# Linear attention and channel mix on one core: pairs of batches against single batches with quarter-tile projections

## Chip, cores, metric

One core of one Trainium2 chip. The time is device microseconds of one execution, as a median of several; the profile is one execution of the same program, and "span" is its length without the fixed cost around it (about 2 us less than the time: 107.7 against 109.86). "Slow" is here a run over 1.5% above the fastest of the same kernel.

## The reference, cut to what matters

```python
# B=4, H=4, S=1088, D=32, r=8; d_model=128, d_ff=1024
def phi(x):                                   # sketch features, 64 per token and head
    a = einsum('rd,bhsd->bhsr', S1, x)
    b = einsum('rd,bhsd->bhsr', S2, x)
    return einsum('bhsi,bhsj->bhsij', a, b).reshape(..., r * r)
q_p, k_p = phi(q), phi(k)
kv, z = einsum('bhsf,bhsd->bhfd', k_p, v), k_p.sum(axis=2)
x = (q_p @ kv) / (q_p @ z + 1e-6)             # heads side by side: (B, S, 128)
xk = mu_k * x + (1 - mu_k) * x_prev           # x_prev: the token before
xr = mu_r * x + (1 - mu_r) * x_prev
out = sigmoid(xr @ w_r) * (relu(xk @ w_k) ** 2 @ w_v)
```

Nothing of q can be finished for a batch before all of its k and v have been summed. So there is an opening (k projection, k features, accumulation of kv and z, q projection, q features, numerators) before the first matmul of the channel mix ("the MLP").

## The kernel before: the parts that matter

The four batches are worked in two halves of two. A tile is 128 rows: two batches by 64 tokens. The k projection is one 128 x 128 by 64-column fp32 matmul per tile, the q projection two half-array ones. The accumulation of kv uses quarters of the array (64 x 64).

```python
def k_proj(half, gi):
    ...
    for t in range(t1 - t0):
        nc.tensor.matmul(p[:, t * 64:t * 64 + 64], kT[half][:, t0 + t, :], SW[:, 0, :, :2, :], ...)

def q_proj(g):
    ...
    for t in range(qn[g]):
        for b2 in range(2):
            nc.tensor.matmul(p[64 * b2:64 * b2 + 64, t * 96:t * 96 + 96], qT[half][:, T, 64 * b2:64 * b2 + 64],
                             SW[:, 2 * half + b2]..., tile_position=(0, 64 * b2))
```

k of the first half and q of the second are transposed on VectorE, the other two on TensorE, after a regrouping on ScalarE. PSUM is four rings of two. A list scheduler in the program orders all pieces; it is told when each load arrives. "Spins" are matmuls of zeros, put there in the hope that they keep the TensorE clock from being lowered.

```python
arrive = {"S": 4.6, "k00": 5.5, "k01": 5.5, "v0": 8.5, "k1": 11.5, "q0": 14.5, "v1": 17.5, "q10": 20.0, "q11": 22.0, "w": 27.0}
...
def spin(count):
    for _ in range(count):
        nc.tensor.matmul(zps[:, 0, :], zero[:, :P], zero[:], skip_group_check=True)
spin(7)   # ... and spin(12) after the small matmuls that prepare the sketch weights
```

## Time and profile before

| | before |
|---|---|
| time, median of the rounds beside the changed kernel | 108.06 us (later rounds: 106.8 to 107.2) |
| span of the profiled run | 107.7 us |
| first MLP matmul starts at (timeline) | 52.1 us |
| from there to the end | 55.6 us |

The profiled run before took 109.86 us and is slow.

TensorE has one hole, and the clock falls twice, near 20 and near 30 to 36 us. The hole, in the timeline of the kernel before (start, length, engine, line, operation, count, and the idle time before it with what ended it): ScalarE waits for a load, TensorE for ScalarE.

```profile
15.24 1.16 PE L227 MATMUL kv<-tok_v_66,kp 64*64 64x64 f32 x64
19.32 1.14 ACT L182 COPY tall<-tok_k_68 128x512 f32<-128x512 f32 x2 [5.05 <-DMA tok_k_68<-in_k_dram]
19.99 1.11 PE L187 MATMUL tp<-ident,tall 128*128 128x128 f32 x4 [3.59 <-ACT tall L182]
```

The table by windows of the kernel before, cut where the first MLP matmul starts. Columns: window, length, busy us of PE, PEld, DVE, ACT and POOL, each with its records, then granted clock, DMA share, GB/s.

```profile
0.00:30.00 30.00, 23.75 (x368) 17.22 (x368) 13.78 (x35) 7.45 (x17) 8.30 (x21) 0.94 0.89 236
30.00:52.10 22.10, 20.39 (x411) 17.53 (x413) 17.31 (x37) 12.47 (x31) 2.31 (x13) 0.85 0.12 13
52.10:107.70 55.60, 50.82 (x586) 36.83 (x594) 46.73 (x90) 50.37 (x78) 0.00 (x0) 1.00 0.12 42
```

Before the MLP, VectorE and ScalarE are idle half of the time; after it PE and ACT are full. This is the room that the change goes after.

### The profile page before, as it was taken

To read this page: it belongs to the slowest core of one execution; us is meant where nothing else is said; L and a number is where in the kernel's file an instruction comes from. 1 tells how busy PE (TensorE), PEld (TensorE's weight loads), DVE (VectorE), ACT (ScalarE), POOL (GpSimd) and SP (SyncE) were. 2 spreads that over 40 slices of the span, in tenths; PEclk is the share of its full clock that TensorE was granted. 3 is DMA by queue.
4 is the path that set the end of the run, shared out by engine and by line. 5 is a ranking of instruction groups with operands and counts; after the bars stand their busy time and mean duration, and the time that the engine had idled before them with its cause. 6 is when DMAs were issued, how large, how long until landed. Compare 5 with 4: busy or idle time off the path is not lost.

```text
span 107.7 us, 3217 instructions
## 1 busy us (share of the span) xinstructions
PE 95.0 (88%) x1365; PEld 71.6 (66%) x1375; DVE 77.8 (72%) x160; ACT 70.3 (65%) x124; POOL 10.6 (10%) x33
## 2 busy tenths in 40 slices
PE   5999990598789999976999999999999999999850
PEld 2445990487679889754667687776866776677720
DVE  3275690123549796949999998599997997878770
ACT  0500410830293533767699999989999998999940
POOL 7050000007790000000000000000000000000000
PEclk9999999679955699999999999999999999999999
DMA  0999999994990000000000000200202002122221
GB/s 10 343 293 366 279 280 287 209 272 159 127 98 0 0 6 6 3 6 0 3 0 6 0 0 0 97 6 0 97 6 97 0 8 90 30 73 97 97 100 53
DMA packets 6157, 9.70 MB, mean 90 GB/s; under 512 B 1520, under 2 KB 2416, under 8 KB 6144
## 3 DMA queue, kind: packets, MB, share of 16 engines
q1 hardware_dynamic: 3360, 6.13, 18.9%
q0 software_dynamic: 1952, 1.71, 8.7%
q10 hardware_dynamic: 832, 1.67, 4.9%
q8 instruction: 11, 0.18, 0.7%
q14 instruction: 2, 0.02, 0.1%
HBM read 7.80 MB, written 2.23 MB: 93 GB/s over the span
## 4 chain that ended last, share of the span: by engine, by line
PE 50%; DMA 19%; ACT 13%; issue 5%; POOL 4%; DVE 3%; SPq 3%; ACTq 0%; POOLq 0%
DMA tok_v_67<-in_v_dram 19%; PE o L419 10%; PE h L398 8%; PE xps L361 8%; PE qtp L323 7%; PE abwp L294 7%; PE tp L187 3%; PE kv L227 3%; PE abp L198 2%; SPq L71 2%; ACT r L435 1%; ACT PP_179 L379 1%; DVE osb L440 1%; ACT k_1507 L404 1%; PE rps L427 1%
## 5 line engine op out<-in xcount | busy, mean ns | idle before, releaser
L398 PE MATMUL h<-XK,wk 128*128 128x512 bf16 (+1 forms) x62 | 17.6, 366 | 0.2
L206 DVE TENSOR_TENSOR kp<-ab 128x1024 f32<-128x1024 f32 (+1 forms) x10 | 10.4, 1060 | 6.5 <-ACT ab L168 6.5
L187 PE MATMUL tp<-ident,tall 128*128 128x128 f32 x34 | 6.9, 340 | 4.1 <-ACT tall L182 4.1
L323 PE MATMUL qtp<-ident,qp 128*128 128x128 f32 x68 | 9.4, 275 | 1.1 <-ACT abw L168 1.0
L206 DVE TENSOR_TENSOR qp<-abw,an 128x1024 f32<-128x1024 f32 (+1 forms) x9 | 10.3, 1154 | 0.0
L168 ACT COPY qpT<-qtp 128x512 f32<-128x512 f32 x15 | 8.3, 601 | 2.4 <-PE qtp L323 2.3
L361 PE MATMUL xps<-qpT,kvbd 128*64 128x256 f32 (+3 forms) x80 | 9.3, 358 | 0.5 <-ACT qpT L168 0.5
L84 PE MATMUL zps<-zero 128*128 128x512 bf16 x19 | 7.6, 578 | 1.3 <-POOL zero L79 1.3
L323 PEld LDWEIGHTS qtp<-ident,qp 128*128 128x128 f32 x68 | 7.4, 142 | 1.6 <-ACT abw L168 1.2
L168 ACT COPY ab<-abp 128x256 f32<-128x256 f32 (+1 forms) x8 | 2.8, 352 | 8.8 <-PE abp L198 8.7
L187 PEld LDWEIGHTS tp<-ident,tall 128*128 128x128 f32 x34 | 4.7, 172 | 4.9 <-ACT tall L182 4.3
L398 PEld LDWEIGHTS <-wk 128*128 128x128 bf16 x72 | 5.8, 98 | 2.5 <-issue 1.0
L361 PEld LDWEIGHTS xps<-qpT,kvbd 128*64 128x64 f32 x80 | 4.5, 136 | 3.2 <-ACT qpT L168 0.7
L198 PE MATMUL abp<-SW,kT_160 128*128 128x64 f32 x34 | 5.5, 304 | 1.0 <-issue 1.0
L440 DVE TENSOR_TENSOR osb<-o,r 128x512 f32<-128x512 f32 (+1 forms) x9 | 5.9, 655 | 0.5 <-PE o L419 0.5
L198 PEld LDWEIGHTS abp<-SW,kT_160 128*128 128x128 f32 x34 | 5.1, 225 | 1.6 <-issue 1.6
L182 ACT COPY tall<-tok_k_68 128x512 f32<-128x512 f32 (+1 forms) x5 | 2.7, 556 | 5.1 <-DMA tok_k_68<-in_k_dram 5.1
L227 PE MATMUL kv<-tok_v_66,kp 64*64 64x64 f32 x272 | 5.9, 244 | 0.0
L84 PEld LDWEIGHTS <-zero 128*128 128x128 bf16 x19 | 2.4, 135 | 5.3 <-issue 3.6
L227 PEld LDWEIGHTS kv<-tok_v_66,kp 64*64 64x64 f32 x272 | 5.2, 155 | 0.8 <-DVE kp L206 0.3
L435 ACT ACTIVATE r<-rps 128x512 f32<-128x512 f32 (+1 forms) x9 | 5.5, 610 | 0.0
L168 ACT COPY abw<-abwp 128x384 f32<-128x384 f32 x6 | 2.9, 482 | 3.4 <-PE abwp L294 3.4
(246 smaller groups left out, 220.2 us busy)
## 6 DMA issues: line engine op xcount, KB each, us to landing
out_dram<-osb SPq DMA_DIRECT2D x7, 256.0 KB, 2.0
hd_k_70<-in_k_dram SPq DMA_DIRECT2D x1, 544.0 KB, 4.0
hd_k_71<-in_k_dram ACTq DMA_DIRECT2D x1, 544.0 KB, 6.0
tok_v_66<-in_v_dram SPq DMA_DIRECT2D x1, 544.0 KB, 8.6
tok_v_66<-in_v_dram ACTq DMA_DIRECT2D x1, 544.0 KB, 9.3
tok_k_68<-in_k_dram SPq DMA_DIRECT2D x1, 544.0 KB, 14.5
tok_k_68<-in_k_dram ACTq DMA_DIRECT2D x1, 544.0 KB, 16.5
tok_q_69<-in_q_dram SPq DMA_DIRECT2D x1, 544.0 KB
```

The lines of the kernel that those rows point to most:

```text
L84: nc.tensor.matmul(zps[:, 0, :], zero[:, :P], zero[:], skip_group_check=True)
L168: nc.scalar.copy(o, i)
L187: nc.tensor.transpose(tp[:, t * P:t * P + P], tall[x, t0][:, t].rearrange("p h d -> p (h d)"), ident[:])
L198: nc.tensor.matmul(p[:, t * 64:t * 64 + 64], kT[half][:, t0 + t, :], SW[:, 0, :, :2, :], skip_group_check=True)
L206: nc.vector.tensor_mul(o, _ap(a_, list(a_.ap[1:]) + [[0, R]]), _ap(b_, list(b_.ap[1:3]) + [[0, R]] + [b_.ap[3]]))
L227: nc.tensor.matmul(kv[hp:hp + 64, b2, (h // 2) * 64:(h // 2) * 64 + 64], f[rows, t - t0, h].rearrange("p i j -> p (i j)"), _ap(rhs, [[(H - ...
L294: nc.tensor.matmul(p[64 * b2:64 * b2 + 64, t * 96:t * 96 + 96], qT[half][:, T, 64 * b2:64 * b2 + 64], SW[:, 2 * half + b2].rearrange("p h ...
L323: nc.tensor.transpose(p[:, t * P:t * P + P], qp[g][:, t, 2 * pair:2 * pair + 2].rearrange("p h i j -> p (h i j)"), ident[:])
L361: nc.tensor.matmul(o[64 * pair:64 * pair + 64], kvbd[:, 2 * half + b2, pair, :], qpT[g, pair][:].rearrange("p t (b s) -> p t b s", b=2)[:, ...
L398: nc.tensor.matmul(h[:, c, :n * P], wk[:, cp, c * P:c * P + P], XK[:, 4 * g:4 * g + n, :].rearrange("p t s -> p (t s)"))
L419: nc.tensor.matmul(bank["o", g][:, t * P:t * P + P], k2[:, c, t * P:t * P + P], wv[:, 2 * cp + c, :], start=(cp == 0 and c == 0 and t == 0 ...
L440: nc.vector.tensor_mul(o[:, :n].rearrange("p t f -> p (t f)"), bank.pop(("o", g))[:, :n * P], rs[g][:, :n * P])
```

## The change

Its intent: work batch by batch, so that the first MLP matmul needs the three loads of one batch and not those of both halves; no TensorE transposes of inputs; a q or k projection cut into quarter-array matmuls, meant to run side by side; PSUM as eight single banks, each piece placed by hand; and 18 spins in places where TensorE was expected to wait. The order of all pieces is a fixed list.

```diff
-    zps = psum.tile([P, 2, 512], F32, name="zps", tag="h")
-    def spin(count):
+    banks = [psum.tile([P, 512], F32, name=f"bank{i}", tag=f"bank{i}") for i in range(8)]
+    def spin(i, count):
...
+    load_v(0)
+    load_kq("q", 0)
+    for b in range(1, B):
+        load_kq("k", b)
+        load_v(b)
+        load_kq("q", b)
...
-    spin(12)
+    spin(0, 5)
...
-        for t in range(t1 - t0):
-            nc.tensor.matmul(p[:, t * 64:t * 64 + 64], kT[half][:, t0 + t, :], SW[:, 0, :, :2, :], skip_group_check=True)
+    def k_proj(b, t0, t1):
+        for t in range(t0, t1):
+            for y in range(2):
+                rows = slice(64 * y, 64 * y + 64)
+                for x in range(2):
+                    nc.tensor.matmul(bank("ab", b, t0, y)[64 * x:64 * x + 64, (t - t0) * 16:(t - t0) * 16 + 16],
+                                     kqT["k", b][rows, t, :], SW[rows, 0, x, :2, :],
+                                     skip_group_check=True, tile_position=(64 * y, 64 * x))
...   (q_proj likewise, 24 columns)
+    ORDER = """
+        tk.0.0.0 tk.0.1.0 kpj.0.0@01 tk.0.0.9 tk.0.1.9 kpj.0.9@23 kab.0.0.0:DVE kab.0.9.1:ACT kab.0.0.1:DVE
+        kab.0.9.0:ACT kp.0.0 spin.6@4 kacc.0.0@45 kp.0.9 kacc.0.9 tk.1.0.0 tk.1.1.0 kpj.1.0@67 tq.0.0.A tq.0.1.A
+        tq.0.1.B kz.0 tq.0.0.B kab.1.0.0:ACT kab.1.0.1:ACT kkv.0 kw.0@0 ksw.0 spin.2@1 q1.0.8@13 q1.0.0@26 qab.0.0.0:ACT
...   (some 40 lines more)
```

In fp32 each of these matmuls is four records on TensorE (two weight loads, two matmuls).

## The prediction

> **What bounds it now.** Engine sums of the page: PE 95.0 us busy, DVE 77.8, ACT 70.3 of a 107.7 us span. Three stages (table by windows, timeline):
> - 0 to 30 us, opening. First K-projection at 10.0 us; PE has nothing from 16.4 to 20.0 us (ACT waits 5.1 us for the second k load), DVE is busy 13.8 of 30 us. Loads cover pairs of batches; the last holds the weights back (POOL waits 17.2 us, issues them at 25 to 28 us). The chain of waits gives that load 19%.
> - 30 to 52 us: both attention halves stand before the MLP. Granted clock 0.84, then 0.67 (20 to 40 us): 64 accumulation records take 1.9 us cold, 1.09 warm. First MLP matmul at 52.1 us.
> - 52 to 104.5 us, steady: PE 50.9 and ACT 50.4 of 52.5 us, DVE 46.4; PE and ACT limit it together, PSUM in rings of two. PE durations overlap, so its 97% is not peak.
>
> **Removed.** 34 PE transposes of k1/q0 (warm 110 ns each by spacing, 3.7 us), ten ACT regroupings (about 4.5 us), ten evacuations (2.5 us ACT, 2.8 DVE). Denominators go from 9 to 5 calls (DVE -2.8). Four squares leave DVE (-2.5) for ACT (+3.7).
>
> **Added.** DVE transposes for the other four batch tensors: +3.3 us. More q evacuations on DVE: +4.5. ACT: 72 half-size relus instead of 36, but back-to-back copies start 0.48 us apart at 512 columns and relus 0.91 at 1024, so only +1.6; more edge pieces, +2.5. Projections: 272 quarter-tile matmuls, two records each, for k and for q. [...] Quarter tiles overlap: the accumulation runs 17 ns a record. At 17 each projection set costs 9.2 us[...]. Spins: 19 become 30; the 18 late ones stand before known waits and keep the clock.
>
> Sums afterwards: ACT about 65, DVE 78, useful PE 80 to 86 us warm. No engine loses much work; the gain is overlap.
>
> **Critical path.** Batch 0 needs three loads (about 1.7 us each at the 290 to 340 GB/s of the DMA row). Walking the order with trace durations (estimate): k projection at 8 us, accumulation done 14, q projection 16.5 to 19, first features 22.5, first numerator 25, x_mix 30, first MLP matmul at 31 to 33 us instead of 52. Then remain PE 55 to 60, DVE 55, ACT 54 us. They balance; with 90 to 95% kept they end near 93 to 95, plus the last MLP chain and store: span 96.
>
> **Prediction: 97.5 us, 8 in 10 within 92 to 103.** Faster by over 2%: 0.93; within 2%: 0.05; slower: 0.02.
>
> **What will show it.** First relu near 32 us; weights issued by about 15 us; granted clock near 1.0 from 12 to 40 us; projection sets of 136 records in 2.3 to 3.7 us; DVE busiest or level with PE, above 85% from 15 us on; ACT no longer saturated.
>
> **What would make it wrong.** Quarter-tile projections whose neighbours share array rows (the accumulation alternates rows) not overlapping:[...] time 105 or above. A fixed order whose guesses are off[...]. DVE transposes of 544 columns costing more than the 0.5 us I extrapolate. The other way: a steady stage without ring waits could run at 97% and give 92.

In the trace of the kernel before, warm, the k projections of all four batches are 68 matmul records 101 to 110 ns apart, 6.9 to 7.5 us, and the q projections 136 records 42.3 ns apart, 5.8 us. The forecast of time is no sum of these terms: the walk to a first MLP matmul at 31 to 33 us, then 55 to 60 us of the busiest engine at 90 to 95%, then the last chain and store, came to a span of 96 us and a time of 97.5. The 80 to 86 us of useful PE contain the projections. The 0.5 us for a transpose of 544 columns is an estimate from the kernel before (0.38 us at 256 columns, 0.40 at 288); the changed kernel took 0.68 us.

## More of the kernel before

The page of the kernel before: busy sums, TensorE's busy tenths in 40 slices of 2.7 us, the granted clock in tenths, and two of the DMA queues (packets, MB, share of 16 engines).

```profile
PE 95.0 (88%) x1365; PEld 71.6 (66%) x1375; DVE 77.8 (72%) x160; ACT 70.3 (65%) x124; POOL 10.6 (10%) x33
...
PE   5999990598789999976999999999999999999850
...
PEclk9999999679955699999999999999999999999999
...
q1 hardware_dynamic: 3360, 6.13, 18.9%
...
q8 instruction: 11, 0.18, 0.7%
```

## The result

| | before | after |
|---|---|---|
| time, median (range) | 108.06 us (107.15 to 110.02) | 120.3 us (119.71 to 121.44) |
| ratio of fast runs | | 1.1177, interval 1.1025 to 1.1328 |
| span of the profile | 107.7 us | 118.5 us |
| first MLP matmul | 52.1 us (a slow run; 48.6 in the fast run of before_kv) | 50.2 us (predicted 31 to 33) |
| from there to the end | 55.6 us | 68.3 us (predicted about 64) |
| TensorE records (PE and PEld) in the trace | 2758 | 4586 |

A ratio is the mean time of one kernel's fast runs over the mean of the other's of the same rounds, so it is not quite the ratio of the medians. The profiled run after is fast. Set against the fast profile of before_kv (48.6 us, then 55.8), nearly all of the loss lies after the first MLP matmul, 12.5 us of some 14; but there about 64 us had been forecast, and the opening was to make up for it.

The same lines of the page, after:

```profile
PE 102.4 (86%) x2284; PEld 73.5 (62%) x2284; DVE 80.6 (68%) x163; ACT 68.9 (58%) x167; POOL 16.1 (14%) x44
...
PE   5999991689987999999697899999999996998900
...
PEclk9999999855586569959999999999999999999995
...
q8 instruction: 18, 0.29, 1.0%
```

The chain that ended last, by engine: first before, then after.

```profile
PE 50%; DMA 19%; ACT 13%; issue 5%; POOL 4%; DVE 3%; SPq 3%; ACTq 0%; POOLq 0%
```

```profile
PE 71%; ACT 10%; issue 7%; DVE 4%; DMA 2%; SPq 1%; POOL 0%; DVEq 0%; POOLq 0%
```

The load that was 19% of the chain is gone, as intended; TensorE's own queue took its place. The table by windows, cut at the changes of the granted clock inside the opening, then the whole from 50.2 us on:

```profile
8.00:16.20 8.20, 8.20 (x199) 6.00 (x202) 5.82 (x13) 0.43 (x2) 6.89 (x9) 1.00 0.98 360
16.20:23.10 6.90, 3.48 (x229) 3.35 (x221) 0.66 (x4) 0.00 (x0) 1.93 (x6) 1.00 1.38 275
23.10:33.30 10.20, 9.53 (x290) 8.65 (x290) 6.22 (x10) 2.31 (x10) 1.71 (x14) 0.50 0.41 41
33.30:36.70 3.40, 3.08 (x155) 2.68 (x148) 2.53 (x7) 1.39 (x6) 0.00 (x0) 1.00 0.03 7
36.70:43.50 6.80, 6.07 (x31) 2.64 (x30) 5.16 (x8) 1.60 (x6) 0.00 (x0) 0.50 0.01 2
43.50:50.40 6.90, 6.62 (x290) 5.33 (x287) 1.98 (x6) 4.84 (x14) 0.00 (x0) 0.99 0.02 5
...
50.20:118.50 68.30, 58.97 (x1112) 42.07 (x1110) 54.23 (x99) 57.02 (x130) 0.00 (x0) 0.95 0.14 35
```

Read it by the second row: from 16.2 to 23.1 us TensorE works half of the time, and VectorE and ScalarE together 0.66 us. They wait for TensorE; what does TensorE wait for? (The 1.00 of the first row is only the absence of a clock record before 16.23 us, where the first one in this trace begins; spins of 512 columns start 427 ns apart there and 216 ns in stretches recorded as full clock, so the clock was half.) The list of waits on TensorE between 12 and 30 us answers with its longest line (the only other one is 0.7 us, at the q projection):

```profile
PE bank_73 L204 <- issue: 3.4, 1, 3.4
```

L204 is the k projection of batch 1. "issue" means that no semaphore that the profile shows was waited for. The operands were there: the same projection had been running since 17.4 us when it stopped. The stop is in the middle of a run of equal matmuls.

Counting the trace's TensorE records in order of start, and noting the packets on the queue q8, I found the regularity (times in us; "idle" is counted from the start of the record before, so that the 3.62 here is the 3.4 of the list above):

```
record        reached at   packet on q8     next block's first record runs at   idle before it
193  (after)  10.23        13.38 to 14.33   449 at 16.29                        0.00
449           16.29        19.40 to 20.37   705 at 21.75                        3.62
705           21.75        24.09 to 25.47   961 at 26.85                        0.93
961           26.85        27.96 to 28.92  1217 at 30.29                        0.05
1217          30.29        31.42 to 32.65  1473 at 34.01                        0.53
1473          34.01        35.15 to 36.13  1729 at 37.47                        0.95
2497          54.95        55.65 to 56.67  2753 at 57.92                        1.10
```

The stops stand at records 193 + 256n. All 18 packets on q8 are of 16,384 bytes, and 4586 records have 18 such edges; the kernel before has 2758 records, 11 edges and 11 packets, `half` and `half_bf16` (below) have 3499 and 2944 records, 13 and 11 edges, 13 and 11 packets. So I read a packet as the next block of 256 TensorE instructions (64 bytes each, as an estimate: 16,384 by 256), and its coming as the fetch of that block. In the rows of the table the packet is on the queue 0.70 to 3.15 us after the block before it is entered: record 449 was reached at 16.29 us, and the packet that 705 waited for came at 19.40. (Outside the table some packets come before the edge, by 1.08 us at most: record 2241 of the kernel before.) In every row but the first, the first record of the new block runs 1.25 to 1.38 us after its packet is through: from 16.3 to 37.5 us each new block is used as soon as it can be. From entering a block to using the next takes 5.1 and 5.5 us here while the loads fill the DMA engines (DMA share 1.38 from 16.2 to 23.1 us; up to 8.0 us in a later run), and 3.0 to 3.7 us when few loads are left. Quarter-tile projections run through 256 records in about 1.9 us (14.7 ns from one matmul record to the next, warm, each with its weight load). So they outrun the fetch: 3.62 us of standing at one crossing.

### The profile page after: what moved, and what is told of

Its sections match the earlier page's. It is cut to its first block, busy times and chain, and to the rows that moved or that the text cites. A ratio compares the mean times of both kernels' runs of the same rounds, so it can differ in the third digit from the quotient of the medians.

```text
span 118.5 us, 5142 instructions
## 1 busy us (share of the span) xinstructions
PE 102.4 (86%) x2284; PEld 73.5 (62%) x2284; DVE 80.6 (68%) x163; ACT 68.9 (58%) x167; POOL 16.1 (14%) x44
## 3 DMA queue, kind: packets, MB, share of 16 engines
q1 hardware_dynamic: 7984, 8.92, 22.5%
## 4 chain that ended last, share of the span: by engine, by line
PE 71%; ACT 10%; issue 7%; DVE 4%; DMA 2%; SPq 1%; POOL 0%; DVEq 0%; POOLq 0%
PE bank_70 L226 5%; PE bank_66 L81 5%; PE bank_66 L226 3%; PE bank_67 L289 3%; PE bank_66 L411 3%; PE bank_68 L358 3%; PE bank_72 L358 2%; DMA out_dram<-osb 2%; PE bank_70 L81 2%; PE bank_70 L389 2%; PE bank_69 L411 2%; PE bank_72 L289 2%; PE bank_68 L204 2%; PE bank_73 L389 2%; PE bank_72 L81 2%
## 5 line engine op out<-in xcount | busy, mean ns | idle before, releaser
L187 DVE TENSOR_TENSOR qp<-abw,an 128x1024 f32<-128x1024 f32 (+7 forms) x12 | 10.4, 909 | 0.1
L389 PEld LDWEIGHTS <-wk 128*128 128x128 bf16 x72 | 6.5, 102 | 6.3 <-issue 3.7
L187 DVE TENSOR_TENSOR kp<-ab 128x1152 f32<-128x1152 f32 (+1 forms) x8 | 10.0, 1286 | 0.3 <-ACT ab L182 0.3
L81 PEld LDWEIGHTS <-zero 128*128 128x128 bf16 x30 | 3.8, 143 | 5.9 <-issue 4.4
L81 PE MATMUL bank_66<-zero 128*128 128x512 bf16 x12 | 5.5, 630 | 1.3 <-POOL zero L77 1.3
L289 PEld LDWEIGHTS bank_72<-SW,kqT 64*64 64x64 f32 x168 | 6.0, 152 | 0.8 <-ACT k_1503 L396 0.8
L289 PE MATMUL bank_72<-SW,kqT 64*64 64x24 f32 x168 | 6.2, 226 | 0.0
L389 PE MATMUL bank_70<-XK,wk 128*128 128x512 bf16 x13 | 5.2, 401 | 1.1 <-DVE XK L378 1.1
L289 PEld LDWEIGHTS bank_67<-SW,kqT 64*64 64x64 f32 x104 | 4.3, 164 | 2.4 <-DVE SW L245 0.8
L389 PE MATMUL bank_73<-XK,wk 128*128 128x512 bf16 (+1 forms) x14 | 5.5, 389 | 0.0
L204 PE MATMUL bank_73<-SW,kqT 64*64 64x16 f32 x68 | 2.3, 205 | 3.4 <-issue 3.4
L289 PE MATMUL bank_67<-SW,kqT 64*64 64x24 f32 x104 | 4.7, 236 | 0.7 <-issue 0.7
L204 PE MATMUL bank_67<-SW,kqT 64*64 64x16 f32 x104 | 4.5, 226 | 0.9 <-issue 0.9
L204 PEld LDWEIGHTS bank_67<-SW,kqT 64*64 64x64 f32 x104 | 4.2, 165 | 1.0 <-issue 1.0
L289 PE MATMUL bank_69<-SW,kqT 64*64 64x24 f32 x104 | 4.5, 236 | 0.0
L289 PEld LDWEIGHTS bank_69<-SW,kqT 64*64 64x64 f32 x104 | 4.1, 164 | 0.5 <-issue 0.5
L204 PEld LDWEIGHTS bank_73<-SW,kqT 64*64 64x64 f32 x68 | 2.2, 135 | 3.5 <-issue 3.5
L204 PE MATMUL bank_68<-SW,kqT 64*64 64x16 f32 x100 | 4.2, 225 | 0.0
```

Source lines behind the costliest of these rows:

```text
L81: nc.tensor.matmul(banks[i][:], zero[:, :P], zero[:], skip_group_check=True)
L187: nc.vector.tensor_mul(o, _ap(a_, list(a_.ap[1:]) + [[0, R]]), _ap(b_, list(b_.ap[1:3]) + [[0, R]] + [b_.ap[3]]))
L204: nc.tensor.matmul(bank("ab", b, t0, y)[64 * x:64 * x + 64, (t - t0) * 16:(t - t0) * 16 + 16], kqT["k", b][rows, t, :], SW[rows, 0, x, :2, :],
L289: nc.tensor.matmul(bank("q", b, r0, y)[64 * x:64 * x + 64, (r - r0) * 24:(r - r0) * 24 + 24], kqT["q", b][rows, t, :], SW[rows, b, x].rear ...
L389: nc.tensor.matmul(bank("h", g, c)[:, :n], wk[:, c // 2, (c % 2) * P:(c % 2) * P + P], XK[:, 8 * g:8 * g + qn[g], :].rearrange("p t s -> p ...
```

## Theories

- F, fetch: the opening is held by the number of TensorE instructions, because blocks come at one per 5.1 to 6.1 us (rows 1 to 3 above; up to 8.0 in a later run) while the loads run.
- C, clock: the projections have only 16 and 24 columns. The theory is that stretches full of them bring the clock down to half (granted 0.50 from 23.1 to 33.3 and from 36.7 to 43.5 us); the cold time costs the rest. It is a guess to be tested: the trace shows the clock, and not what sets it.
- S, spins: the 18 late spins delay what stands behind them in TensorE's order (about 7 us of TensorE time, part of it where nothing was to be waited for: features ready at 12.30 us, the accumulation begun behind six spins at 14.67).
- M, found on the way: VectorE waits for a memset on GpSimd that stands behind the landing of the weights (7.8 us in bf16q, below).

## The experiments

Eighteen kernels ran. Each entry gives the edit and the result. All outputs were correct except where an entry says otherwise. "MLP at" is the start of the first MLP matmul in that kernel's profiled run. Those of nolate, wide, half, half_nop, mix1, arr3_fill, pw and bf16q_pw were slow runs; I use them for where the stops stand, and times and ratios for how much a version costs.

### nolate: no late spins

```diff
-kp.0.0 spin.6@4 kacc.0.0@45 ... ksw.0 spin.2@1 q1.0.8@13 ... qp.0 spin.1@2 qt.0@21 ... spin.5@6 num.0@6 ... (and 4 more)
+kp.0.0 kacc.0.0@45 ... ksw.0 q1.0.8@13 ... qp.0 qt.0@21 ... num.0@6 ...
```

> The changed kernel without its 18 late zero matmuls; nothing else differs. Theory S (the spins themselves delay TensorE, which takes its queue in order: 2.67 us before the first accumulation, 0.87 before the first q projection, 2.15 before the first numerator): 4 to 6 us faster than the changed kernel's 120.3, first MLP matmul at 45 to 46 us instead of 50.2. Theory C (the clock decides[...]): the clock stays at half until past 20 us, the first accumulation and the second k projection run at 28 ns a record instead of 20, and the gain shrinks to 0 to 3 us.

Measured: 117.8 us, ratio 1.0907 (1.0885 to 1.0929); MLP at 48.1 us. So some 3 us of the loss are S, less than the spins' own 7 us. Records now come to the block edges sooner and wait there; but the clock was also at half from 10.9 to 31.3 us of that run, as the other expectation had it (in the changed kernel it was full from 16.2 to 23.1). How the missing 4 us divide between the two was not tested. The stops stood at 449 (2.26 us), 705 (2.48) and 961 (1.70), the same record numbers, though every instruction after the removed spins had moved up.

### wide: the same quarter tiles, zero-padded to 64 columns

```diff
-bank("ab", b, t0, y)[..., (t - t0) * 16:(t - t0) * 16 + 16], kqT["k", b][rows, t, :], SW[rows, 0, x, :2, :]
+bank("ab", b, t0, y)[..., (t - t0) * 16:(t - t0) * 16 + 64], kqT["k", b][rows, t, :], SWk[rows, x]  # zeros behind
```

> The changed kernel with the moving operand of every quarter-tile projection widened from 16 or 24 columns to 64 with zero columns (the surplus results are overwritten or never read); same instructions, same order, same spins. Theory C[...]: the windows that fell to half clock during projections (23 to 33, 36.7 to 43.5, 50.3 to 53.8 us) are mostly at full clock, the first q projection goes from 29 to about 17 ns a record, the first MLP matmul comes 5 to 9 us earlier, total 111 to 115 us. Rival (the low clock comes from TensorE's pauses alone, the fetch gap and waits): clock rows unchanged, total 119 to 122 us, since a 64-column stream costs as much as the accumulation already does.

Measured: 117.2 us, ratio 1.093 (1.0899 to 1.0961); MLP at 50.7 us. The half-clock windows of 36.7 to 40 and 50.4 to 53.8 us are gone (half only at 20.2 to 33.9 and 40.7 to 44.1), the stop at record 705 is as long as before:

```profile
21.15 2.61 PE L207 MATMUL bank<-SWk,kqT 64*64 64x64 f32 x82 [3.83 <-issue]
```

The padded records follow each other in 16.2 ns (113 from 35.32 us, full clock), the same ones unpadded in 14.5 (34.01 us of the changed kernel), the accumulation's in 14.8 (43.72 us there). By the time, padding is worth about 3 us by fast runs, which is neither expectation (111 to 115, or 119 to 122). Where they are gained is not shown: the profile is of a slow run that took 120.02 us, as long as the changed kernel. In it the first MLP matmul came no earlier, and the clock was still at half from 20.2 to 33.9 us, so this run does not say what C costs in the opening.

### early8: 8 early spins instead of 5

```diff
-    spin(0, 5)
+    spin(0, 8)
```

> The changed kernel with 8 instead of 5 zero matmuls before the first k projection[...]. Theory C: full clock from 9.4 us instead of 16.2; the first k projection starts 1.2 us later but runs at 17 ns instead of 28 ns a record, the six spins after it take 1.3 instead of 2.7 us, the first accumulation ends at 15 to 16 instead of 17.6 us; total 0 to 3 us faster. Rival ([...]the order's waits decide): total 0 to 1.5 us slower, by the added spins.

(The 9.4 us is where the clock record of the kernel before, with 7 and then 12 early spins, begins: full from 9.34 us.) Measured: 120.7 us, ratio 1.1265 (1.1211 to 1.1318; the changed kernel 1.1177, 1.1025 to 1.1328, so no difference); MLP at 50.3 us. The clock was full from 10.1 us, the first projection ran at 16.4 ns from record to record instead of 26.4, and the gain was swallowed whole: record 705 ran at 22.04 us, against 21.75.

### hold: the loads of batches 2 and 3 issued later

```diff
-    for b in range(1, B):          # all loads at the start
+    for b in range(1, 2):          # batches 2 and 3 after kz.0
```

> The changed kernel with the six loads of batches 2 and 3 issued only after a one-element DVE write that follows kz.0 (about 17.7 us), so that the queues are nearly empty when TensorE's next block of instructions is fetched at 16 to 20 us. Theory F (the 3.4 us gap in the second k projection at record 705 is a late instruction fetch queued behind the input loads): the gap shrinks to 0.5 to 1.8 us, the clock does not fall at 23 us, total 3 to 6 us faster. Rival (the gap has another cause, or is the bare latency of a fetch): the gap stays at 3 us or more, total within 1.5 us of 120.3. The later gaps at records 961, 1729 and 2753 should stay at 0.7 to 1.1 us under either.

Measured: 121.1 us, ratio 1.1281 (1.1233 to 1.1329); MLP at 51.9 us. The fetch behind record 449 became quicker (4.3 us from edge to use instead of 5.5) and the stop at 705 shrank from 3.4 to 1.6 us, as F said. The next fetch met the held loads and took 7.3 us, with stops of 1.8 and 1.7 us at 961 and 1217: the DMA work was moved, not removed. The gain of 3 to 6 us that F forecast is a miss. The clock was at half from 15.3 to 46.0 us of this run, so its time says little about F alone.

### half: the quarter tiles undone

Two matmuls with all 128 rows and 32 (k) or 48 (q) columns per tile instead of four quarters; order and spins as in the changed kernel.

```diff
-            for y in range(2):
-                rows = slice(64 * y, 64 * y + 64)
-                for x in range(2):
-                    nc.tensor.matmul(..., kqT["k", b][rows, t, :], SW[rows, 0, x, :2, :], tile_position=(64 * y, 64 * x))
+            for x in range(2):
+                nc.tensor.matmul(..., kqT["k", b][:, t, :], SW[:, 0, x::2, :2, :], tile_position=(0, 64 * x))
```

> The changed kernel with its quarter-tile projections undone alone: each 64-token tile is projected with two 128-row matmuls (one per column half, 32 or 48 columns) instead of four 64-row ones; order, spins, banks and everything after the projections stay. TensorE records fall by 544 matmuls and 544 weight loads, from about 4590 to 3500. Theory F (the opening is paced by fetching TensorE's instructions, 256 records at a time, 5 to 7 us each while loads run): the first MLP matmul comes after 7 blocks instead of 9 to 10, at 40 to 44 us instead of 50.2; total 109 to 114 us. Rival Q (array time decides): a projection set costs 3.5 us warm instead of 2.3, eight sets are 8 to 10 us more array work, total 121 us or more.

Measured: 112.1 us (109.75 to 112.53; three of four runs count as slow, so there is no ratio); MLP at 45.95 us; 13 instruction packets and 3499 records instead of 18 and 4586. By the medians, eight of the thirteen lost microseconds came back: the first MLP matmul came 4.3 us earlier, and the rest after it took 64.6 us instead of 68.3. The array time did not change: fully warm, half-tile records follow each other in 28.6 ns, quarter-tile records in 14.6, and there are twice as many. Here 32 columns became 16, the array time stayed, and the number of instructions doubled.

### half_nolate and half_early8_nolate

`half` without the 18 late spins, and the same with 8 early spins.

```diff
-kp.0.0 spin.6@4 kacc.0.0@45 ... (all late spins, as in nolate)
+kp.0.0 kacc.0.0@45 ...
-    spin(0, 5)      # half_early8_nolate only
+    spin(0, 8)
```

> The same without the 18 late spins. If the fetch pace was what made the spins nearly free (without them TensorE only waited longer: 2.3 us gained of 5.7 removed), they should now cost more of their length: 3 to 5 us faster than half. If they pay for themselves by the clock, the difference is under 1.5 us.

Measured: 111.5 us, ratio 1.0449 (1.037 to 1.0528); MLP at 44.6 us.

> Half-tile projections, no late spins, 8 instead of 5 early ones. Theory C+F: with the fetch no longer the pace, full clock from about 9.4 us shortens the first projection and accumulation, 0 to 2 us faster than half_nolate. Rival: 0 to 1.5 us slower, by the spins.

Measured: 111.0 us, ratio 1.0372 (1.027 to 1.0475); MLP at 44.9 us. Small steps, the first not the 3 to 5 us expected; the opening still stood at 45 us.

### mix1 and mix2: half tiles in the opening, quarter tiles after it

Half tiles for batches 0 and 1, quarter tiles for 2 and 3; no late spins, 8 early ones; three output buffers instead of two; the memsets of M early. mix2 also holds back loads and weights.

```diff
+            if b < 2:      # in k_proj and q_proj: as in half
+                ...
+                continue
-        o = work.tile([P, 4, P], F32, name="osb", tag="osb", bufs=2)
+        o = work.tile([P, 4, P], F32, name="osb", tag="osb", bufs=3)
-    nc.gpsimd.tensor_copy(warm[:], kq["k", 0][:R, 0, 0, :1])      # mix2 only: weights later,
+    nc.gpsimd.tensor_copy(warm[:], kq["q", 1][:R, 0, 0, :1])      # and the loads of batches 2, 3 as in hold
```

> A first attempt at a better version: half-tile projections for batches 0 and 1 only (the opening, where instruction fetch paces TensorE), quarter tiles for batches 2 and 3 (where array time counts: 2.3 us a set against 3.5), no late spins, 8 early ones, the small constant fills on GpSimd ahead of the weight loads (DVE waited 3.1 us for one behind the last weight in the half-tile runs), three output buffers instead of two (the last product waited 1.4 us for a store). If fetch, the late constant and the array time are as read: 2 to 4 us less than half_early8_nolate's 111.0, at 107 to 109.5 us. If the quarter tiles of batches 2 and 3 bring the fetch gaps back: no gain.

Measured: 111.65 us (109.53 to 116.93), ratio 1.0336 (1.0222 to 1.045); MLP at 43.6 us. A miss: within the noise this is half_early8_nolate, not 2 to 4 us less. The stop at record 449 was still 4.0 us, and one of 1.0 us stood at 1217.

> mix1 with the loads of batch 2 issued after kz.0, those of batch 3 after qp.0, and the weights after the loads of batch 1, so that the first instruction fetches find emptier queues. Theory F: the block of records 449 to 705 is usable 2 to 3 us sooner, the first MLP matmul comes 2 to 4 us earlier than in mix1, 104 to 107 us. Rival: as in hold, a later fetch meets the held loads instead and the sum is unchanged within 1.5 us.

Measured: 115.4 us, ratio 1.0778 (1.0679 to 1.0877); MLP at 46.8 us. Holding loads back lost again. The first fetch, with emptier queues, took 3.5 us from edge to use and its stop shrank to 1.3 us; two later fetches met the held loads and stopped TensorE 3.3 and 3.5 us.

### half_nop: a test that did not take place

`half` with two no-ops after each projection matmul, to bring back the number of instructions without array work.

```diff
                                  skip_group_check=True, tile_position=(0, 64 * x))
+                for _ in range(2):
+                    nc.tensor.nop(nofuse=True)
```

> The half-tile projections of the run 'half' (112.1 us), with two sequencer no-ops[...] after each projection matmul, 1088 in all, so that TensorE has again the instruction count of the changed kernel but none of its quarter-tile array work. Instruction-fetch theory: the stream again needs about 18 instruction packets of 16 KB; stretches without a visible releaser of 1 to 4 us come back at block boundaries between 16 and 27 us, the first MLP matmul comes at 49 to 51 us (half: 45.9) and the time is 117 to 120 us. Rival (the quarter tiles cost by their own array time[...], not by their number): 14 packets or whatever the count is, no longer stops, first MLP matmul within 1 us of 45.9, time 111.5 to 113. A mixed result (114 to 116) would split the loss between the two. If a no-op itself takes over 20 ns of the queue, the no-ops add over 20 us of sequencer time and the test is spoiled; the record spacing in the projections will show it.

Measured: 110.9 us (108.86 to 111.32); MLP at 44.4 us. The no-ops were dropped when the program was built: 13 packets and 3499 records, as in `half`. So this was a repeat of `half` on another chip, and useful only as that: the two medians are 112.1 and 110.9.

### before_kv: two memsets of the old kernel moved up

```diff
+    kvbd = const.tile([P, B, 2, 2 * D], F32)      # now ahead of the wait for the last v load
+    nc.gpsimd.memset(kvbd[:], 0.0)
+    pws = ...; memset
```

> The kernel before with two memsets on GpSimd (block-diagonal kv tile and the two denominator tiles) moved ahead of the wait for the last v load. In the profile of before, ScalarE waited 3.67 us for that memset at 25.3 to 28.9 us, with two regroupings of k1 and q0 behind it. If the opening of the old kernel is bound by that chain: the first MLP matmul comes 1 to 3 us before 52.1 us and the time is 105 to 106.5 (ratio 0.98 to 0.99). If TensorE's clock and the order after it bind: within 0.5 us of before, ratio 0.995 to 1.005.

Measured: 106.6 us, ratio 0.9952 (0.9895 to 1.001). The wait of 3.67 us is gone from ScalarE, and half a per cent of the time with it (1 at most, by the interval; the verdict is unclear): that opening is bound elsewhere.

### arr3: the old kernel with true arrival times

```diff
-    arrive = {..., "k1": 11.5, "q0": 14.5, "v1": 17.5, "q10": 20.0, "q11": 22.0, "w": 27.0}
+    arrive = {..., "k1": 17.5, "q0": 19.5, "v1": 22.5, "q10": 23.5, "q11": 24.5, "w": 28.0}   # and before_kv
```

> As before_kv, and the six arrival times that the old kernel's list scheduler is told (k1 11.5, q0 14.5, v1 17.5, q10 20, q11 22, weights 27) set to what the trace shows less the scheduler's offset of about 1.7 us (17.5, 19.5, 22.5, 23.5, 24.5, 28). The order then puts the last three accumulations of half 0 ahead of the k1 transposes, into TensorE's empty stretch of 16.4 to 20.0 us. Theory 'a fixed order stands on its arrival times': gap of 3.6 us falls below 1.5, the 256-column accumulations all done by 20 us instead of 25.4, no half-clock window at 19.6 to 23.0, first MLP matmul at 47 to 50 us, time 102 to 106 (ratio 0.95 to 0.985). Rival (the old steady stage absorbs it, or its tuned keys fit only the old order): 106 to 109, ratio 0.99 to 1.02, with new waits after the first MLP matmul.

Measured: 110.9 us, ratio 1.0369 (1.0293 to 1.0444; the record classes it as unclear, though the interval lies above 1): no gain, and probably a loss. The order did as intended, the accumulations follow each other without a break. But here is TensorE's timeline of that run (start, length, engine, line, operation, count, idle before it):

```profile
13.95 1.16 PE L229 MATMUL kv<-tok_v,kp 64*64 64x64 f32 x64
15.04 0.43 PE L200 MATMUL abp<-SW,kT 128*128 128x64 f32 x2
15.40 1.73 PE L229 MATMUL kv<-tok_v,kp 64*64 64x64 f32 x99
21.75 3.26 PE L229 MATMUL kv<-tok_v,kp 64*64 64x64 f32 x109 [4.62 <-issue]
```

The stop is at record 449, in a kernel without one quarter-tile projection. The old kernel has the same packet (record 193 reached at 14.32, the packet on the queue 18.67 to 19.98 us) and never showed it: its order made TensorE wait for ScalarE from 16.4 to 20.0 us, so the fetch was hidden behind a wait that I took for waste: its record 449 ran at 21.84 us, without a stop, 1.86 us after the packet was through. (At the next edge, record 705, the old kernel did stop, for 1.04 us, until 1.42 us after its packet was through.) The stop is not the whole loss: against before_kv, which has the same memsets, the first MLP matmul came 2.4 us later (51.07 against 48.63), and 2.2 us more were lost after it (58.0 against 55.8), as the rival had it. The cause of that second part was not looked for.

### bf16q: quarter tiles kept, instructions halved

The projections read the upper halves of the same fp32 tiles as bf16, so a matmul is two records and not four (the q projection of one batch, 17 tiles by four quarters, stands in the trace as 68 matmul records; in the changed kernel as 136). Its output is wrong, which doesn't matter for the time.

```diff
-kqT["k", b][rows, t, :], SW[rows, 0, x, :2, :]
+hi(kqT["k", b][rows, t, :])[:, 1::2], hi(SW[rows, 0, x, :2, :])[:, :, 1::2]     # hi: the tile seen as bf16
```

> The changed kernel with its order, spins and quarter-tile shapes kept, but the k and q projections read the upper halves of the same fp32 tiles as bf16 (wrong result on purpose: truncated operands, and the denominators are sensitive). A matmul is then two records instead of four: 1088 fewer, as many as 'half' has, with the narrow shapes (16 and 24 columns) kept[...]. Fetch theory: 13 or 14 instruction packets instead of 18; the stop at record 705 gone or moved as in 'half' (one stop of 3 to 4 us at record 449); first MLP matmul at 43 to 47 us; time 108 to 113. Clock and narrowness theory: the half-clock windows of the changed kernel stay (half until 16 us, 23 to 33, 37 to 44), first MLP matmul at 48 to 50 us, time 115 to 119.

Measured: 111.8 us, ratio 1.048 (1.0417 to 1.0543); MLP at 44.8 us; 13 packets. The shapes are as narrow as in the changed kernel and the granted clock is much the same (0.877 to 0.901 in its fast runs, 0.864 to 0.900 in those of the changed kernel; `half` had 0.924 to 0.984 in all its runs), yet the time is that of `half`. What `half` and `bf16q` have in common is the number of instructions. bf16q also spends less array time in its projections (a warm q set took 0.72 us from first start to last end, at 42.67 us; 2.18 in the changed kernel, at 54.16; in `half` 68 records at 28.6 ns, 1.9 us), and gained nothing by it: TensorE stood instead, at records 449, 705 and 961.

```profile
15.45 0.38 PE L229 MATMUL bank<-vt,kp 64*64 64x64 f32 x3 [3.85 <-issue]
21.37 0.45 PE L292 MATMUL bank<-SW,kqT 64*64 64x24 bf16 x20 [2.00 <-issue]
27.39 0.64 PE L229 MATMUL bank<-vt,kp 64*64 64x64 f32 x26 [2.64 <-issue]
```

F had forecast one stop as in `half`, so this detail is a miss, but the time, the packets and the first MLP matmul are as F said and not as C said. F holds against C for these 8 us.

That they wait for the fetch still is supported by when record 961 was reached, the fourth edge, in nine versions whose work up to that record differs (half_nop is `half` again):

```
after 26.85   nolate 26.13   early8 27.31   wide 27.90   hold 25.70   half 28.33   half_nop 27.38   bf16q 27.39   half_pw 27.28
```

The versions left out lie at 26.85 (pw, bf16q_pw), 27.26 (half_nolate), 27.90 (mix2), 28.77 (half_early8_nolate) and 30.77 (mix1). So the number of records done by about 27 us depends little on what they do (half_bf16, below, had run out of work and reached it at 39.98). What differs is how far in the program record 961 lies: in the changed kernel in the q projection of batch 0, in `half` near the end of batch 1's accumulation.

### half_bf16: fewer instructions still

```diff
-kqT["k", b][:, t, :], SW[:, 0, x::2, :2, :]           # in half
+hi(kqT["k", b][:, t, :])[:, 1::2], hi(SW[:, 0, x::2, :2, :])[:, :, :, 1::2]
```

> The half-tile version ('half', 112.1 and, repeated, 110.9 us) with the same bf16 reading of the projections (wrong result on purpose): 544 records fewer than 'half', 1632 fewer than the changed kernel. Fetch theory: the stop of 3.4 to 3.7 us at record 449 falls on a later piece of work or shrinks, first MLP matmul 1 to 3 us before 45 us, time 108 to 110.5. If after the quarter tiles nothing of the fetch is left to save, the gain is only the array time of the 8 projection sets[...]: time 109 to 111, first MLP matmul within 1.5 us of 'half'.

Measured: 113.0 us, ratio 1.0585 (1.0504 to 1.0667), result wrong as above; MLP at 46.5 us; 2944 records. A miss: 544 instructions fewer, and nothing gained. The stops shrank (2.77, 0.57 and 1.64 us), but VectorE then stood 8.4 us before the first denominators, and TensorE was at half clock from 19.4 to 39.8 us. The limit had moved to M. In bf16q M is the longest of VectorE's waits between 20 and 34 us:

```profile
DVE den L309 <- POOL pw L276: 7.8, 1, 7.8
```

Why the memset is so late, GpSimd's timeline of the changed kernel shows, where the order on that engine is the same:

```profile
29.52 0.61 POOL L261 TENSOR_SCALAR wr_c<-wr_f,mu_r 128x128 bf16<-128x128 f32 x1 [11.38 <-DMA wr_f<-in_moe_w_r_dram]
30.12 0.59 POOL L262 TENSOR_SCALAR wr_p<-wr_f,omu_r 128x128 bf16<-128x128 f32 x1
30.66 0.15 POOL L273 MEMSET pw_187<- 128x34 f32 x1
```

It stands behind two products that need the weight `wr_f`, and that wait is 11.38 us long.

### arr3_fill: 128 more instructions ahead of arr3's opening

```diff
-    spin(7)
+    spin(1)
+    for i in range(70):
+        y, x = i // 2 % 2, i % 2
+        nc.tensor.matmul(zps[64 * x:64 * x + 64, y, :16], zero[64 * y:64 * y + 64, :64], zero[64 * y:64 * y + 64, :16], ...)
```

> The reordered old kernel arr3 (110.9 us; its accumulation stopped 4.84 us at record 449, 16.9 to 21.75 us, without any quarter tile in it), with 6 of its first 7 spins replaced by 70 tiny zero matmuls, so that 128 more instructions stand ahead of the first projection, in a stretch where TensorE has nothing else to do. Nothing after them changes. Fetch theory: record 193 is crossed at about 11 us instead of 14.5, the block of record 449 comes 2.5 to 3.5 us earlier, the stop falls from 4.8 to 0.5 to 2.5 us, half 0's accumulation ends at 20.5 to 22.5 us instead of 24.9, time 107 to 109.5: more instructions, faster. Rival (the stop is not the fetch but a late wait or the clock): the stop stays at the same place in the accumulation, 110.5 to 111.5 us.

Measured: 112.9 us, ratio 1.0545 (1.0469 to 1.0621). Half a hit. The stop at record 449 vanished, as F said it must. It came back one block later, at 705, longer:

```profile
15.85 2.66 PE L233 MATMUL kv<-tok_v,kp 64*64 64x64 f32 x163
24.35 1.55 PE L233 MATMUL kv<-tok_v,kp 64*64 64x64 f32 x45 [5.85 <-issue]
```

In arr3 the accumulation had done 64 + 99 = 163 matmul records before the stop, here 2 + 62 + 163 = 227. The difference, 64 matmul records with their 64 weight loads, is 128: exactly 256 less the 128 instructions put in. A wait in the program would have stayed at its matmul; this one stays at its record number. What I had wrong is the size: this block took 8.0 us from edge to use (on the queue 21.40 to 22.77 us), where I had reckoned with 5 to 7.

### pw, half_pw, bf16q_pw: the memset moved ahead of the weight loads

```diff
+    pw = ...; memset; kvbd = ...; memset       # now before the weight loads on GpSimd
     mu_k = const.tile([P, 1], F32)
```

> The changed kernel with one thing moved: the memsets of the denominator tiles and of the block-diagonal kv tile stand on GpSimd ahead of the weight loads. In the profile of the changed kernel the q features of batch 0 reach VectorE at 30.7 us and the memset is done at 30.8 us, so both end together. If the instruction fetch and the rest of TensorE's queue bind there: 119 to 121 us, ratio 1.11 to 1.125, first MLP matmul at 49.5 to 50.5 us. If the memset bound: first MLP matmul 1 us or more earlier, time 117 to 119.

Measured: changed kernel with this alone, 120.3 us (117.97 to 121.26); MLP at 48.5 us in a run that took 119.94. No ratio, since the fast run stands alone; the median is that of the changed kernel. The first denominators start at 31.16 us, before at 31.11: the memset did not bind there, TensorE came as late. The MLP did start 1.7 us earlier, which the expectation had tied to the memset; but in that run the clock was at half for 3.4 us between 37.7 and 41.1, where the changed kernel has 6.8 us (36.7 to 43.5), and the median total is the same.

> The half-tile version without late spins and with 8 early ones (half_early8_nolate, 111.0 us, ratio 1.037), the memsets moved ahead of the weight loads, and three output buffers instead of two. If the memset is the next limit of the opening: the first denominators at 27 to 28 us instead of 31, first MLP matmul at 42 to 43.5 us instead of 44.9, time 108.5 to 110, ratio 1.015 to 1.03. If not: 110.5 to 111.5, ratio 1.03 to 1.04.

Measured: 108.9 us (106.62 to 110.65; one fast run, so no ratio); denominators at 25.8 us, MLP at 40.1 us.

> bf16q (111.8 us; wrong result on purpose, as before) with the memsets moved ahead of the weight loads. There the q features of batch 0 were ready at about 23 us and VectorE waited 7.8 us. If the memset is the next limit: the first denominators at 23 to 25 us, the first MLP matmul at 39 to 42 us instead of 44.8, time 107 to 110. If TensorE's queue order and clock bind (its order puts batch 1's k work ahead of the first transposes): first MLP matmul within 1.5 us of 44.8, time 110.5 to 112.5.

Measured: 106.6 us, ratio 0.9981 (0.9934 to 1.0028), result wrong as above; denominators at 24.4 us, MLP at 42.5 us in its profile (a slow run of 109.52). So M was the next limit once the instructions were fewer, worth about 5 us in bf16q (fast runs: 111.6 to 106.6) and 2 to 4 us in half tiles (111.0 to a median of 108.9, or to the one fast run of 106.62; the third output buffer is in the same edit). Without the fewer instructions it gave nothing in the median (pw).

The profile of half_pw is of its fast run, and is the best correct opening. Its table by windows, cut at the first MLP matmul:

```profile
20.00:40.07 20.07, 18.26 (x529) 15.80 (x529) 16.27 (x30) 9.79 (x33) 1.54 (x10) 0.87 0.54 49
40.07:104.70 64.63, 56.27 (x906) 41.26 (x905) 54.56 (x101) 56.67 (x130) 0.00 (x0) 0.99 0.14 37
```

Its MLP starts 8.6 us before that of before_kv (48.6 us, fast like this run; 12 us before the old kernel's slow profile), and it ends where the old kernel ends: from there on 64.6 us are left, against 55.8. The batch-wise order leaves the attention of later batches behind the first MLP matmul, and PE (56.3), ACT (56.7) and DVE (54.6) are full from there to the last fin near 100 us. A version that beats both kernels was not found.

## Why the prediction was wrong

**The step that failed** is "Critical path": "k projection at 8 us, accumulation done 14, q projection 16.5 to 19, first features 22.5, first numerator 25, x_mix 30, first MLP matmul at 31 to 33 us". Measured: 8.2, 17.6, q projection done 29.5, features 33.3, numerator 42.8, x_mix 48.9, MLP 50.2 us. I walked the order with the durations of matmuls and never asked whether the instructions themselves would be there. 18 us of the 22.5 us by which the span missed (118.5 against 96) are this step.

**What stood in its place**, by the runs: up to about 37 us TensorE is paced by the fetch of its instructions, one block of 256 in 5.1 to 8.0 us while the loads run. Halving the projections' instructions gave 8 us back (half, bf16q): 4.3 and 5.4 us before the first MLP matmul, some 3.7 us after it. With the instructions halved, a memset behind the weights was next (half_pw: 40.1 us). What then still parts 40.1 from 32 is, as an estimate from half_pw's profile, the stops that remain (3.5, 0.4 and 0.8 us) and half clock from 18.3 to 25.2 us, which costs half of 6.9 us: together 8 us. The two overlap in part, and no run took them away separately.

The fetch is not all of the 18 us in the changed kernel. TensorE stood 5.4 us at block edges in the opening (3.42, 0.67, 0.32, 0.73 and 0.28). Besides, the accumulation was done 3.6 us late before any stop (it began behind six spins at 14.7 us, with features ready at 12.3), and from the first features at 33.3 to the numerator at 42.8 us, 9.5 us where I had put 2.5, TensorE worked, apart from 1.1 us of these stops, through the next batches' pieces and six spins that the order puts first, mostly at half clock. How these divide the rest was not separated: no run kept the clock full through the opening.

**"Then remain PE 55 to 60, DVE 55, ACT 54"** was right: half_pw shows 56.3, 54.6 and 56.7. So was the length of the rest, about 64 us predicted, 64.6 in half, bf16q and half_pw alike. In the changed kernel it was 68.3. As an estimate from its trace, half clock from 50.4 to 53.8 us costs up to 1.7 us of that, and the stop at record 2753 another 1.1; no run separated them.

**"At 17 each projection set costs 9.2 us"**, quarter tiles overlapping: right, 14.6 ns from record to record when fully warm (136 records from 81.45 to 83.42 us), and irrelevant. The risk I named, that they would not overlap, did not come. I asked whether the array could take the instructions at that rate, not whether it would get them.

**"The 18 late ones stand before known waits and keep the clock"**: wrong in the main. The waits were guessed from an order that ran late; k features were ready at 12.30 us, and the six spins ran on in front of the accumulation:

```profile
11.99 2.74 PE L81 MATMUL bank_70<-zero 128*128 128x512 bf16 x6
14.67 0.36 PE L226 MATMUL bank_70<-vt_91,kp 64*64 64x64 f32 x1
```

Without the late spins the kernel was about 3 us faster (nolate), though its clock was then lower from 16 to 23 us. With them the clock was at half from 23.1 to 33.3 and from 36.7 to 43.5 us all the same. Every change of the clock in this trace falls on a grid of 3.41 us (16.23, 23.05, 33.30, 36.71, 43.53, 50.36, 53.77, 115.22 us). What brings it down the trace does not settle: the steps of that grid from 33.3 us (TensorE busy 3.08 of 3.40 us, mostly a k projection of 16 columns) and from 46.9 us (3.14 of 3.42, mostly a q projection of 24) were followed by half clock, the step from 53.8 us (3.25 of 3.41, a q projection of 24 columns and part of a k projection of 16) was not.

**"Granted clock near 1.0 from 12 to 40 us", "VectorE above 85% from 15 us on"**: both wrong, as consequences. VectorE was busy 0.66 us of 6.9 while TensorE stood.

**"Weights issued by about 15 us"**: nearly right (17.3 us), and not the thing to ask: they landed at 29.5 us, and a memset stood behind them.

What stays open: how much of the 8 us from `half` belongs to the fetch alone was not isolated by adding instructions to it (half_nop failed); it rests on bf16q and half agreeing, on the nearly fixed time of record 961, and on the stop that moved with the record number in arr3_fill. Why half_pw spreads over 4 us from run to run is not known.

## What to carry to other kernels

Count TensorE instructions as a resource: before cutting matmuls into smaller ones, compare the records per microsecond of the dense stretches with the pace measured here, one block of 256 per 5.1 to 8.0 us while loads ran and per 3.0 to 3.7 us with few left, and look for "issue" waits in the middle of equal instructions. A hole in a tuned kernel can hide a second limit that shows only when the hole is filled (record 449: no stop in the kernel before, 4.62 us in arr3), so an order laid out from durations alone (arr3, and the change itself) should be checked against instruction count. And an opening that starts the next stage earlier is worth only what the work left behind does not take back.
